# Clustered attention with an MLP: the small products of the q, k, v and x scales in even units behind the scores, and two tiles of the MLP's inner layer in one bank and pass

## The chip, the cores and the metric

The kernel runs on one core of a Trainium2 chip. TensorE (PE) multiplies, VectorE (DVE), ScalarE (ACT) and GpSimd (POOL) work elementwise, SyncE (SP) issues all transfers from one queue, in order. Each engine works through its own instructions in order. The metric is the time of one execution on the device, in microseconds (us); the figure for a kernel is the median of its runs.

## What is computed

Attention in which a query sees only the keys of its own cluster (the nearest of 16 centroids), and an MLP on its result:

```python
batch, n_heads, seq, head_dim = (4, 8, 768, 64)      # n_clusters = 16
q_assign = np.argmax(np.einsum('bhsd,hcd->bhsc', q_n, c_n), axis=-1)
k_assign = np.argmax(np.einsum('bhsd,hcd->bhsc', k_n, c_n), axis=-1)
mask = q_assign[:, :, :, None] == k_assign[:, :, None, :]
scores = scale * np.matmul(q, k.transpose(0, 1, 3, 2))
scores = np.where(mask, scores, -1000000000.0)
attn = softmax(scores)
x = np.matmul(attn, v)          # 3072 tokens x 512
h = x @ w_in                    # w_in 512 x 2048
r = np.maximum(h, 0.0)
out = (s * (r * r) + b) @ w_out # w_out 2048 x 512
```

Here q_n, k_n and c_n are q, k and the centroids divided by their norms. All inputs are float32.

## The kernel before

Float32 numbers are split into two float16 parts, hi and lo, after scaling by a power of two, and products are made of three matmuls of parts. The scale comes from the largest magnitude of a tile. DVE reduces along the free axis into a column `amb`, and a **small product** on PE (`allmax`, tile `am`) brings all 128 columns to every partition, where DVE reduces again.

The main loop runs over **units** i = 0 to 191, one per batch, pair of 128-row tiles of the queries, pair of heads, tile and head (`units`). In the timeline's names: `sc` are the scores of a unit (4 matmuls into one of two banks), `ssm` their maximum on DVE, `p` the exp on ACT, `ph` its hi part (ACT) and lo part (POOL), `PT` its transpose by DMA, `px` the product with v (`values`, in odd units for the two units five and four back), `xs` the divided result. Every four units `finish_x` makes `xn` (the hi and lo parts of `xs`) and its transpose `x`.

The MLP runs 21 units behind (`LAG`): step m = i - 21 takes one 128-wide tile `ft` of the inner layer for 256 tokens. Since 21 is odd, even steps m fall in odd units. `mlp_in` makes `h` (12 matmuls of 256 columns), `mlp_relu` makes `r` and the hi part of `g` on ACT, `mlp_gl` its lo part on POOL a unit later, `mlp_out` adds 6 matmuls of 512 columns into `acc` two units later. After 16 steps DVE makes `o` out of `acc`, and it goes out.

The inputs of later units are made by generators that `background` moves by one step at the end of every unit. `prep_q` (every 8 units), `prep_k` (four per batch) and `prep_v` (one per batch) load, take `absmax`, bring the scale round (`am`), split into hi (ACT) and lo (DVE), transpose (`QA`, `KA`), multiply with the centroids (`pq`, `pk`), make a one-hot row of the nearest on DVE (`om`, `oe`, `oo`, then `qb` or `kb`) and transpose again (`QB`, `KB`). For all pairs of heads after the first batch `kb` is one buffer: POOL copies the hi part of `ka` into it, DVE writes the one-hot beside it, and the KB transpose reads it.

`px`, `pq`, `pk` and `am` share one bank of PSUM (pool `ps_m`, tag m, one buffer). `h` has one bank too (`ps_h`), `acc` two as one buffer.

From unit 21 on (`pinned`) PE, DVE, ACT and POOL keep the order in which the code is written; SP's queue and everything before unit 21 are ordered by a scheduler.

## Time and profile before

| | us |
|---|---|
| median of 3 runs | 985.37 |
| lowest and highest | 985.28, 995.64 |
| profiled execution | 989.84 |
| its span, first to last instruction | 988.1 |
| matmuls on PE | 8625 |
| PE's mean granted clock, share of full | 0.932 |

The prediction shows lines of the profile. In a group of instructions stand the line of the code (L51 is the helper that records most instructions), engine, operation, output and inputs with shapes, count, busy us and mean ns of one, then the idle time of the engine ahead of them and what ended it. In a view of waits stand the waiting engine and tile, what it waited for, the sum in us, how often, and the longest. In a timeline stand start and length in us. A unit is called by its number i; the scores of unit 30 start at 207.16 us, those of unit 79 at 429.56, of 127 at 639.89, and of 191, the last, at 917.35.

### The profile page before, as it was taken

How to read it: one execution, taken by the hardware profiler on the slowest of the kernel's cores; microseconds unless marked ns; L12 is line 12 of the kernel's file. 1: busy time of each engine (PE TensorE's matmuls, PEld its weight loads, DVE VectorE, ACT ScalarE, POOL GpSimd, SP SyncE). 2: the span in 40 equal slices, each digit the busy share in tenths (PEclk: the TensorE clock that was granted, in tenths of full speed). 3: DMA queues.
4: the chain of work that ended last, by engine and by line, in shares of the span. 5: the costliest groups of instructions: out<-in, count | busy, mean ns of one | idle time of the engine just before them, and what ended most of it. 6: DMA issues, size and time to landing. Idle time of an engine off the chain costs nothing. (4 is left out here: it accounts for less than half of the span.)

```text
span 988.1 us, 22624 instructions
## 1 busy us (share of the span) xinstructions
PE 838.5 (85%) x8625; PEld 584.5 (59%) x8625; DVE 656.1 (66%) x1475; ACT 755.0 (76%) x1416; POOL 547.8 (55%) x543
## 2 busy tenths in 40 slices
PE   1576526787989999997899999997899999999997
PEld 0355315555566666675666776765566767667764
DVE  7798878898786655667876665676776556563200
...
GB/s 190 195 196 170 250 209 104 94 140 198 142 148 159 149 144 127 146 158 215 186 147 149 147 130 155 146 192 187 137 154 158 126 140 150 144 136 126 74 28 21
DMA packets 450300, 147.36 MB, mean 149 GB/s; under 512 B 417936, under 2 KB 446608, under 8 KB 450192
## 3 DMA queue, kind: packets, MB, share of 16 engines
...
## 5 line engine op out<-in xcount | busy, mean ns | idle before, releaser
L51 POOL TENSOR_TENSOR ph<-p,ph 128x768 f16<-128x768 f32 x184 | 308.1, 1675 | 80.1 <-ACT ph L51 55.1
L51 PE MATMUL h<-x,wis 128*128 128x256 f16 x2304 | 285.6, 273 | 12.6 <-ACT r L51 6.5
L51 PE MATMUL acc<-wos,g 128*128 128x512 f16 x1152 | 288.1, 387 | 0.8 <-POOL g L51 0.6
L51 POOL TENSOR_TENSOR g<-r,g 128x256 f16<-128x256 f32 x192 | 129.7, 676 | 276.4 <-ACT r L51 270.4
L51 PEld LDWEIGHTS <-wis 128*128 128x128 f16 x2304 | 226.4, 98 | 83.4 <-issue 17.6
L51 DVE TENSOR_REDUCE ssm<-sc 128x1 f32<-128x768 f32 x192 | 182.8, 953 | 102.0 <-PE sc L51 101.3
L51 ACT ACTIVATE p<-sc,ssm,qsm 128x768 f32<-128x768 f32 x192 | 189.9, 989 | 7.9
L51 PEld LDWEIGHTS <-g 128*128 128x128 f16 x1152 | 108.8, 100 | 109.2 <-issue 10.2
L51 ACT ACTIVATE r<-h,cf 128x256 f32<-128x256 f32 x192 | 89.9, 468 | 99.6 <-PE h L51 89.6
L51 ACT ACTIVATE ph<-p 128x768 f16<-128x768 f32 x174 | 143.9, 827 | 1.4 <-DMA KA<-ka 1.4
L51 PEld LDWEIGHTS <-PT 128*128 128x128 f16 x3312 | 117.7, 99 | 32.3 <-issue 22.9
L51 PE MATMUL px<-vh,PT 128*128 128x65 f16 x2208 | 121.2, 197 | 15.3 <-DVE qsm L51 7.9
L51 PE MATMUL sc<-KA,QA 128*128 128x384 f16 x384 | 101.4, 349 | 16.9 <-ACT p L51 14.0
L51 PE MATMUL px<-vl,PT 128*128 128x64 f16 x1104 | 115.1, 195 | 0.0
L51 ACT ACTIVATE ssm<-ssm,lift,qsm 128x1 f32<-128x1 f32 x192 | 72.2, 377 | 52.8 <-DVE ssm L51 51.9
L51 PE MATMUL sc<-KB,QB 128*128 128x384 f16 x384 | 101.8, 350 | 1.9 <-DMA QB<-qb 1.9
L51 ACT ACTIVATE g<-r 128x256 f16<-128x256 f32 x192 | 80.0, 417 | 6.1
L51 ACT ACTIVATE r<-r 128x256 f32<-128x256 f32 x192 | 80.0, 417 | 6.0
L51 PEld LDWEIGHTS <-QA 128*128 128x128 f16 x768 | 48.9, 100 | 28.2 <-issue 20.7
L51 PEld LDWEIGHTS <-QB 128*128 128x128 f16 x384 | 39.7, 104 | 31.2 <-issue 7.1
L51 DVE SCALAR_TENSOR_TENSOR o<-acc,xm,bias 128x512 f32<-128x512 f32 x24 | 16.9, 745 | 44.5 <-PE acc L51 44.4
L51 DVE TENSOR_SCALAR qsm<-qsm 128x2 int32<-128x2 int32 (+1 forms) x96 | 42.8, 446 | 2.2
...
## 6 DMA issues: line engine op xcount, KB each, us to landing
...
PT<-ph SPq DMA_TRANSPOSE x184, 3.5
x<-xn SPq DMA_TRANSPOSE x48, 2.9
```

Of the source, the lines that this page charges most:

```text
L51: ins = op(*args, **kw)
```

## The change

Four things are changed.

- **Where `allmax` stands.** In batches after the first, and for x, it is put on a list `soon` and made in the next unit, right behind the scores. For q and k the step of the generator that came before it is taken out, so that splitting and transposing come a unit earlier, and a step is put in before the products with the centroids, which keep their place in q.
- **Which units.** `prep_k` starts 3 units later, so that `am_k` and `pk` fall in even units, in which there is no `px`. `prep_v` starts 10 units later.
- **x.** `finish_x` is no generator any more. Its hi part and maxima are made in the odd unit, the rest (`am_x`, POOL's lo part, the transpose) stands in `soon`, ahead of POOL's other work of the even unit. It stood at the end of that unit.
- **The MLP in pairs.** In odd units `mlp_in` makes two tiles (24 matmuls) into the two halves of one bank, and one relu of 512 columns reads them. In even units ACT makes two squares of 512 columns, POOL one lo part, now behind `ph` of that unit, and PE the 12 matmuls of the pair before. `r` has one buffer for two, `g` two for four, of double size.

Two small tiles of the set-up (`ct`, `cnat`) change tags to fit.

Three places. First PE around the small product of q in unit 96 (`am_q2_0_1`; the second row of each pair is left out, `sc_97` and `sc_96` are scores). Before:

```order
L51 MATMUL h_1_1_11_7401<-x_19_6447,wis11_2267 128x256
L51 LDWEIGHTS amb_q2_0_1_7378
L51 MATMUL am_q2_0_1_7428<-identb_95,amb_q2_0_1_7378 128x128
L51 LDWEIGHTS QA_2_0_0_6936
L51 MATMUL sc_97_7435<-KA_2_0_6191,QA_2_0_0_6936 128x384
```

Now:

```order
L51 MATMUL sc_96_7075<-KB_2_0_6112,QB_2_0_0_6582 128x384
L51 LDWEIGHTS amb_q2_0_1_7073
L51 MATMUL am_q2_0_1_7083<-identb_95,amb_q2_0_1_7073 128x128
L51 LDWEIGHTS g_1_1_8_6933
L51 MATMUL acc_1_1_6466<-wos8_2031,g_1_1_8_6933 128x512
```

The product moved from the end of the unit to behind its scores, ahead of the 12 matmuls into `acc`.

Second DVE from the division in unit 95 (`xs_22`) to the maximum of the next scores. `amb_q` is what PE's `am_q` reads, `qsm` what DVE makes of it. Before:

```order
L51 TENSOR_TENSOR xs_22_7182<-px_90_7273,ssm_88_6733 128x128
L51 TENSOR_REDUCE om_k2_3_7372<-pk_2_3_7347 128x12
L51 TENSOR_TENSOR oe_k2_3_7373<-pk_2_3_7347,om_k2_3_7372 128x192
L51 TENSOR_REDUCE amb_q2_0_1_7378<-qn_2_0_1_7226 128x2
L51 TENSOR_REDUCE xm_20_6722<-xs_22_7182 128x1
L51 TENSOR_REDUCE ssm_96_7390<-sc_96_7383 128x1
L51 TENSOR_TENSOR oe_k2_3_7373<-oe_k2_3_7373,rev_73 128x192
L51 TENSOR_REDUCE om_k2_3_7372<-oe_k2_3_7373 128x12
L51 TENSOR_TENSOR oo_k2_3_7374<-oe_k2_3_7373,om_k2_3_7372 128x192
L51 TENSOR_SCALAR kb_131<-oo_k2_3_7374 128x12x64
L51 TENSOR_REDUCE qsm_2_0_1_7377<-am_q2_0_1_7428 128x2
```

Now:

```order
L51 TENSOR_TENSOR xs_22_6864<-px_90_6982,ssm_88_6461 128x128
L51 TENSOR_REDUCE xm_20_6428<-xs_22_6864 128x1
L51 TENSOR_TENSOR oe_k2_2_6966<-oe_k2_2_6966,rev_73 128x192
L51 TENSOR_REDUCE om_k2_2_6965<-oe_k2_2_6966 128x12
L51 TENSOR_TENSOR oo_k2_2_6967<-oe_k2_2_6966,om_k2_2_6965 128x192
L51 TENSOR_SCALAR kb_131<-oo_k2_2_6967 128x12x64
L51 TENSOR_REDUCE vm_2_6655<-vn_2_1_6752 128x1
L51 SCALAR_TENSOR_TENSOR ka_2_3_6975<-kn_2_3_6754,ksm_2_0_5981,ka_2_3_6975 128x12x64
L51 TENSOR_REDUCE amb_q2_0_1_7073<-qn_2_0_1_6905 128x2
L51 TENSOR_REDUCE qsm_2_0_1_7072<-am_q2_0_1_7083 128x2
L51 TENSOR_REDUCE ssm_96_7089<-sc_96_7075 128x1
```

The work of k and v that stood in other units now stands between the division and `amb_q`, and the maximum of the next scores stands behind `qsm`.

Third POOL around the copy into `kb` for the third pair of heads of batch 2 (`ka_2_2`). Before, in units 88 and 89:

```order
L51 TENSOR_TENSOR g_1_1_3_6759<-r_1_1_3_6757,g_1_1_3_6759 128x256
L51 TENSOR_TENSOR ph_88_6831<-p_88_6736,ph_88_6831 128x768
L51 MEMSET vh_2_0_6874 128x12x2
L51 COPY kb_131<-ka_2_2_6778 128x12x64
L51 TENSOR_TENSOR g_1_1_4_6862<-r_1_1_4_6860,g_1_1_4_6862 128x256
L51 TENSOR_TENSOR ph_89_6898<-p_89_6835,ph_89_6898 128x768
```

Now, in units 91 and 92:

```order
L51 TENSOR_TENSOR ph_90_6700<-p_90_6598,ph_90_6700 128x768
L51 COPY kb_131<-ka_2_2_6653 128x12x64
L51 TENSOR_TENSOR xn_21_6739<-xs_21_6546,xn_21_6739 128x2x128
L51 TENSOR_TENSOR ph_91_6764<-p_91_6704,ph_91_6764 128x768
L51 TENSOR_TENSOR g_1_1_6_6783<-r_1_1_6_6734,g_1_1_6_6783 128x512
```

The copy stood a unit behind the KB transpose that reads `kb` for the pair before; now both are issued at the end of the same unit. Behind the copy stands `xn`, ahead of `ph`, and `g` of double width at the end.

The core of the diff:

```diff
@@ -337,8 +339,9 @@
         km = columns(1, f"k{n}")
         absmax(km, kn.rearrange("p h t d -> p (h t d)"))
         if b:
-            yield
-        allmax(sm[1], km, f"k{n}", "m" if b or not hp else "h")
+            soon.append(lambda: allmax(sm[1], km, f"k{n}"))
+        else:
+            allmax(sm[1], km, f"k{n}", "h" if hp else "m")
         yield
         scale2(sm[2], sm[1])
         inverse2(V, sm[3], sm[2], 22)
...
@@ -353,6 +356,8 @@
         KS[(b, hp)] = (KA, KB)
         last_turn[0] = nc.sync.dma_start_transpose(KA, ka.rearrange("p h t e d -> p (h t e d)"))
         yield
+        if b:
+            yield
         yield
         pa = (ps_m if b or not hp else ps_h).tile([P, 512], F32, tag="m" if b or not hp else "h", name=f"pk_{n}")
         for h in range(2):
...
@@ -381,8 +386,9 @@
         qm = columns(2, f"q{n}")
         absmax(qm, qn.rearrange("p (j h) t d -> p j (h t d)", j=2))
         if b + c:
-            yield
-        allmax(sm[:, 1, :], qm, f"q{n}", "m" if b or c else "h")
+            soon.append(lambda: allmax(sm[:, 1, :], qm, f"q{n}"))
+        else:
+            allmax(sm[:, 1, :], qm, f"q{n}", "h")
         yield
         f = sm[:, 2, :]
         scale2(f, sm[:, 1, :])
...
@@ -405,6 +411,8 @@
         QS[(b, c, hq)] = (QA, QB, sm)
         nc.sync.dma_start_transpose(QA, qa.rearrange("p h t e d -> p (h t e d)"))
         yield
+        if b + c:
+            yield
         yield
         pa = (ps_m if b or c else ps_h).tile([P, 512], F32, tag="m" if b or c else "h", name=f"pq_{n}")
         for h in range(nh):
...
@@ -441,8 +449,9 @@
         vc = columns(1, f"v{b}")
         V.tensor_reduce(vc, vm[:, 0:NP], axis=AX.X, op=ALU.max)
         if b:
-            yield
-        allmax(vm[:, 5:6], vc, f"v{b}")
+            soon.append(lambda: allmax(vm[:, 5:6], vc, f"v{b}"))
+        else:
+            allmax(vm[:, 5:6], vc, f"v{b}")
         yield
         floor2(V, vm[:, 6:7], vm[:, 5:6])
         inverse2(V, vm[:, 7:8], vm[:, 6:7], 0)
...
@@ -570,16 +579,20 @@
         xn = sb.tile([P, CT, 2, 2, D], F16, tag="xn", name=f"xn_{g}", bufs=1)
         A.activation(xn[:, :, 0], xs, AF.Copy)
         absmax(XM[(b, c)][:, hp : hp + 1], xs.rearrange("p t h d -> p (t h d)"))
-        yield
-        G.tensor_tensor(xn[:, :, 1], xs, xn[:, :, 0], op=ALU.subtract)
-        x = sb.tile([P, CT, 2, P], F16, tag="x", name=f"x_{g}", bufs=9)
-        XS[(b, c, hp)] = x
-        nc.sync.dma_start_transpose(x.rearrange("p t e q -> p (t e) q"), xn.rearrange("p t e h d -> p (t e h d)"))
+        xm = XM[(b, c)]
         if hp == NP - 1:
-            xm = XM[(b, c)]
             xc = columns(1, f"x{g}")
             V.tensor_reduce(xc, xm[:, 0:NP], axis=AX.X, op=ALU.max)
-            allmax(xm[:, 5:6], xc, f"x{g}")
+
+        def rest():
+            if hp == NP - 1:
+                allmax(xm[:, 5:6], xc, f"x{g}")
+            G.tensor_tensor(xn[:, :, 1], xs, xn[:, :, 0], op=ALU.subtract)
+            x = sb.tile([P, CT, 2, P], F16, tag="x", name=f"x_{g}", bufs=9)
+            XS[(b, c, hp)] = x
+            nc.sync.dma_start_transpose(x.rearrange("p t e q -> p (t e) q"), xn.rearrange("p t e h d -> p (t e h d)"))
+
+        soon.append(rest)
 
 
     MS = {}
...
@@ -597,28 +610,34 @@
         V.scalar_tensor_tensor(xm[:, 7:8], xm[:, 6:7], xm[:, 6:7], glob[:, 6:7], op0=ALU.mult, op1=ALU.mult)
         MS[(b, c)] = [cf, xm[:, 7:8], None]
 
+
     def mlp_in(b, c, ft):
         n = f"{b}_{c}_{ft}"
-        ph = ps_h.tile([P, 512], F32, tag="h", name=f"h_{n}")
+        ph = ps_h.tile([P, 2, CW], F32, tag="h", name=f"h_{n}")
         GS[(b, c, ft)] = ph
         terms = [(kt, wl, xl) for kt in range(KT) for wl, xl in ((0, 0), (0, 1), (1, 0))]
-        for i, (kt, wl, xl) in enumerate(terms):
-            M.matmul(ph[:, :CW], WSP[ft][0][:, wl, kt, :], XS[(b, c, kt)][:, :, xl, :],
-                             start=(i == 0), stop=(i == len(terms) - 1))
+        for f in range(2):
+            for i, (kt, wl, xl) in enumerate(terms):
+                M.matmul(ph[:, f, :], WSP[ft + f][0][:, wl, kt, :], XS[(b, c, kt)][:, :, xl, :],
+                                 start=(i == 0), stop=(i == len(terms) - 1))
 
     def mlp_relu(b, c, ft):
         n = f"{b}_{c}_{ft}"
         ph = GS[(b, c, ft)]
-        r = sb.tile([P, CW], F32, tag="r", name=f"r_{n}", bufs=2)
-        A.activation(r, ph[:, :CW], AF.Relu, scale=MS[(b, c)][0])
-        g = sb.tile([P, 2, CW], F16, tag="g", name=f"g_{n}", bufs=4)
-        A.activation(g[:, 0, :], r, AF.Square)
+        r = sb.tile([P, 2, CW], F32, tag="r", name=f"r_{n}", bufs=1)
+        A.activation(r, ph, AF.Relu, scale=MS[(b, c)][0])
+        GS[(b, c, ft)] = r
+
+    def mlp_square(b, c, ft):
+        r = GS[(b, c, ft)]
+        g = sb.tile([P, 2, 2, CW], F16, tag="g", name=f"g_{b}_{c}_{ft}", bufs=2)
+        A.activation(g[:, 0], r, AF.Square)
         A.activation(r, r, AF.Square)
         GS[(b, c, ft)] = (r, g)
 
     def mlp_gl(b, c, ft):
         r, g = GS[(b, c, ft)]
-        G.tensor_tensor(g[:, 1, :], r, g[:, 0, :], op=ALU.subtract)
+        G.tensor_tensor(g[:, 1], r, g[:, 0], op=ALU.subtract)
         GS[(b, c, ft)] = g
 
     def mlp_out(b, c, ft):
...
@@ -627,12 +646,13 @@
             MS[(b, c)][2] = ps_a.tile([P, CT, DM], F32, tag="acc", name=f"acc_{n}")
         acc = MS[(b, c)][2]
         g = GS.pop((b, c, ft))
-        for t in range(CT):
-            rows = slice(t * P, t * P + P)
-            for gl, wl in ((0, 0), (0, 1), (1, 0)):
-                M.matmul(acc[:, t, :], g[:, gl, rows], WSP[ft][1][:, wl, :],
-                                 start=(ft == 0 and gl + wl == 0), stop=(ft == NF - 1 and gl == 1))
-        if ft == NF - 1:
+        for f in range(2):
+            for t in range(CT):
+                rows = slice(t * P, t * P + P)
+                for gl, wl in ((0, 0), (0, 1), (1, 0)):
+                    M.matmul(acc[:, t, :], g[:, gl, f, rows], WSP[ft + f][1][:, wl, :],
+                                     start=(ft + f == 0 and gl + wl == 0), stop=(ft + f == NF - 1 and gl == 1))
+        if ft == NF - 2:
             _, e, acc = MS.pop((b, c))
             o = sb.tile([P, CT, DM], F32, tag="stage", name=f"o_{n}", bufs=3)
             if b + c == 0:
...
@@ -665,8 +685,8 @@
                     at(s0, prep_q(b, c, hq))
         if b > 0:
             for hp in range(NP):
-                at(48 * b - 20 + 4 * hp, prep_k(b, hp))
-            at(48 * b - 16, prep_v(b))
+                at(48 * b - 17 + 4 * hp, prep_k(b, hp))
+            at(48 * b - 6, prep_v(b))
     splits = wsplit()
     wgen = weights()
 
...
@@ -737,6 +757,8 @@
         if i < NU:
             with first_of_all(i):
                 scores(i)
+        while soon:
+            soon.pop(0)()
         if due:
             with first_of_all(i):
                 px = values(i - 5)
...
@@ -754,18 +776,20 @@
             some(splits, 1)
         if 0 <= m < NS and steps[m][2] == 0:
             mlp_start(*steps[m][:2])
-        if 0 <= m - 2 < NS:
-            mlp_out(*steps[m - 2])
-        if 0 <= m < NS:
+        if m % 2 and 0 <= m - 3 < NS:
+            mlp_out(*steps[m - 3])
+        if m % 2 and 0 <= m - 1 < NS:
+            mlp_square(*steps[m - 1])
+        if m % 2 == 0 and 0 <= m < NS:
             mlp_in(*steps[m])
             mlp_relu(*steps[m])
-        if 0 <= m - 1 < NS:
-            mlp_gl(*steps[m - 1])
         if 0 <= i - 1 < NU:
             with first_of_all(i):
                 low(i - 1)
+        if m % 2 and 0 <= m - 1 < NS:
+            mlp_gl(*steps[m - 1])
         if due and (i - 5) % 4 == 2:
-            active.append(finish_x((i - 5) // 4))
+            finish_x((i - 5) // 4)
         background()
         if i >= LAG - 3:
             some(splits, 1)
```

More of the change, by code (lines that the diff above doesn't have):

```diff
@@ L87, in scale2 @@
         V.tensor_scalar(dst, dst, 2.0 ** 60, None, op0=ALU.min)
+    soon = []
     last_transpose = [None]
@@ L150, in behind @@
         return stack
-    ct = sb.tile([P, 2, D], F32, tag="r", name="ct", bufs=2)
+    ct = sb.tile([P, 2, D], F32, tag="r", name="ct", bufs=1)
     cn = ct[:, 0, :]
@@ L168, in tile_cluster_attention_mlp @@
     V.reciprocal(cs[:, 3:4], cs[:, 2:3])
-    cnat = sb.tile([P, 3, 2, D], F16, tag="r", name="cnat", bufs=2)
+    cnat = sb.tile([P, 3, 2, D], F16, tag="g", name="cnat", bufs=2)
     G.memset(cnat[:, 1:3], 0.0)
```

## The prediction

> **What bounds the kernel now.** I read the page's busy times first, then the windows, PE's waits, and the timeline where PE waits.
>
> ```profile
> PE 838.5 (85%) x8625; PEld 584.5 (59%) x8625; DVE 656.1 (66%) x1475; ACT 755.0 (76%) x1416; POOL 547.8 (55%) x543
> ```
>
> PE is the busiest engine, but it has 150 us without work. The windows tell where. I cut them at starts of scores: set-up; the first MLP steps while the weights are still split (units 21 to 29); then by turns the stretches in which the next batch's k and v are prepared (units 30 to 49, 79 to 97, 127 to 145) and quiet ones; last the tail without attention. Columns: stretch, its length, busy PE, PEld, DVE, ACT, POOL with counts, granted clock, DMA share, GB/s.
>
> ```profile
> 0.00:160.80 160.80, 77.70 (x612) 55.33 (x613) 133.28 (x303) 105.75 (x201) 75.57 (x90) 0.71 0.75 192
> 160.80:207.16 46.36, 37.51 (x386) 26.00 (x387) 39.49 (x74) 37.68 (x68) 25.57 (x22) 0.92 0.53 112
> 207.16:312.23 105.07, 90.06 (x974) 61.36 (x972) 86.14 (x188) 77.48 (x140) 57.71 (x54) 0.98 0.84 161
> 312.23:429.56 117.33, 112.74 (x1217) 79.71 (x1215) 70.23 (x159) 101.02 (x191) 73.04 (x70) 1.00 0.73 143
> 429.56:523.96 94.40, 82.95 (x921) 57.31 (x919) 73.23 (x170) 71.64 (x130) 54.18 (x53) 0.95 0.91 177
> 523.96:639.89 115.93, 112.86 (x1216) 79.66 (x1214) 70.92 (x159) 100.89 (x191) 73.07 (x70) 1.00 0.72 144
> 639.89:738.77 98.88, 85.78 (x920) 58.23 (x918) 73.31 (x169) 71.69 (x130) 54.74 (x53) 0.91 0.87 165
> 738.77:917.35 178.58, 174.27 (x1876) 123.45 (x1873) 100.91 (x230) 155.09 (x293) 113.10 (x107) 1.00 0.75 142
> 917.35:988.10 70.75, 64.63 (x523) 43.44 (x520) 8.60 (x25) 33.73 (x76) 20.78 (x28) 1.00 0.15 36
> ```
>
> Set-up is DVE's (133 of 160.8 us busy). In quiet stretches PE is 96 to 98% busy: nothing but PE's own work is left there. In the two later preparations PE is 87 to 88% busy, the clock falls to 0.95 and 0.91, and DVE is busiest after PE. What PE waited for from 160.8 us on:
>
> ```profile
> PE pk L51 <- DVE xs L51: 12.7, 7, 3.3
> PE am_x L51 <- DVE amb_x L51: 12.2, 10, 2.3
> PE px L51 <- DVE qsm L51: 7.9, 5, 2.2
> PE am_k L51 <- DVE oe_k L51: 7.6, 9, 0.8
> PE h L51 <- ACT r L51: 6.5, 6, 1.5
> PE h L51 <- DMA x<-xn: 6.1, 7, 1.5
> PE am_q L51 <- DVE ksm L51: 2.9, 3, 1.3
> ```
>
> The first four and the last are one thing: px, pk, pq and am all use bank m, and each must wait until DVE has read the one before. A quiet pair of units on PE:
>
> ```profile
> 361.76 0.49 PE L51 MATMUL sc<-KA,QA 128*128 128x384 f16 x2
> ...
> 362.41 1.46 PE L51 MATMUL acc<-wos,g 128*128 128x512 f16 x6
> 363.70 1.47 PE L51 MATMUL h<-x,wis 128*128 128x256 f16 x12
> 365.01 0.49 PE L51 MATMUL sc<-KA,QA 128*128 128x384 f16 x2
> ...
> 369.36 0.49 PE L51 MATMUL sc<-KA,QA 128*128 128x384 f16 x2
> ```
>
> An even unit takes 3.25 us (361.76 to 365.01): scores 0.65, acc 1.29, h 1.31. An odd one takes 4.35, with 1.1 for the values px. And a bad place:
>
> ```profile
> 451.02 0.75 PE L51 MATMUL pk<-cT,KA 128*128 128x16 f16 x24 [1.57 <-DVE xs L51]
> ...
> 461.00 0.23 PE L51 MATMUL am_x<-identb,amb_x 128*128 128x128 bf16 x1 [2.26 <-DVE amb_x L51]
> ...
> 463.34 2.54 PE L51 MATMUL acc<-wos,g 128*128 128x512 f16 x6
> ```
>
> After such gaps six acc matmuls take 2.54 us, not 1.46: a wait is paid twice. Lost by the clock in the four windows under 1.00 (length times what is missing): 3.7 + 2.1 + 4.7 + 8.9 = 19.4 us.
>
> **The change, part by part.** The profiled execution took 989.8 us for a span of 988.1; the median of the three runs is 985.4, so I make the sum on 989.8 and take 4.4 off at the end.
>
> *Two tiles of the inner layer in one bank and pass.* PE's matmuls keep number and size: 24 h in an odd unit (2.6 us), 12 acc in an even one (2.6), so 3.25 + 4.35 per pair as before. It saves on ACT and POOL:
>
> ```profile
> L51 ACT ACTIVATE r<-h,cf 128x256 f32<-128x256 f32 x192 | 89.9, 468 | 99.6 <-PE h L51 89.6 <-DVE om_q L51 3.3 <-PE am_k L51 1.8
> L51 ACT ACTIVATE g<-r 128x256 f16<-128x256 f32 x192 | 80.0, 417 | 6.1
> L51 ACT ACTIVATE wo<-wo 128x512 f32<-128x512 f32 x16 | 10.0, 622 | 6.8 <-DVE wo L51 6.8
> L51 POOL TENSOR_TENSOR ph<-p,ph 128x768 f16<-128x768 f32 x184 | 308.1, 1675 | 80.1 <-ACT ph L51 55.1 <-issue 4.6 <-DVE xs L51 3.0
> L51 POOL TENSOR_TENSOR g<-r,g 128x256 f16<-128x256 f32 x192 | 129.7, 676 | 276.4 <-ACT r L51 270.4 <-issue 5.4 <-PE px L51 0.4
> ```
>
> A 512-wide pass costs 622 ns where two narrow ones cost 834: about 0.2 us for the relu and 0.4 for the two squares in each of 96 pairs, 60 us of ACT; 512-wide g on POOL is halfway between 676 and 1675, 1.18 for 1.35, 17 us. Neither engine ends the path in quiet stretches, so I cost this at nothing; PE covers it, and without that cover it would be a gain. By the Trainium skill, "ScalarE: Activation LUTs", section on what ACT_TABLE_LOAD costs, a pass has a fixed 186 ns and 0.833 per element, an estimate of 613 for 512; the wo row agrees. "h waits for r" (6.5) falls in units 22 to 28. The bank now has an even unit and the next scores and px to come free (5 us, not 2). But DVE was busy 39.5 of 46.4 us there, and the wider h needs split weights a unit earlier: between 0 and 6.5 I take 2.2, near DVE's bound. r with one buffer: the relu waits for g on POOL, which ends about 3 us ahead in a quiet pair; no cost. Tail: last relu, two squares and g (0.7 + 1.24 + 1.18, some 0.4 between) stand against 2.6 of acc: +1.
>
> *x first.* am_x goes behind the scores of the even unit, at 0.65; its columns are ready some 3 us into the 4.35 of the odd one. The 12.2 go, from both kinds of stretch. POOL's xn stands ahead of ph (1.68) and g, so x lands earlier by more than the 1.5 that h waited: I take 5 of 6.1.
>
> *Small products in even units.* pk leaves the odd units, where it waited for the px just ahead: 12.7 go. am_k stands ahead of pk, not behind: 7.6 go. px behind am_q: 7.9 go, and the 2.9 of am_q. Together with the above 50.5 us of waits leave. Set-up: am and xn move a little under a scheduler; DVE bounds it (83% busy) and its work stays: 0, give or take 5.
>
> *What is late next.* am now stands ahead of 2.6 us of acc that would have covered it. What it waits for is DVE's queue:
>
> ```profile
> L51 DVE TENSOR_REDUCE ssm<-sc 128x1 f32<-128x768 f32 x192 | 182.8, 953 | 102.0 <-PE sc L51 101.3
> L51 DVE TENSOR_TENSOR xs<-px,ssm 128x128 f32<-128x128 f32 x96 | 27.9, 291 | 9.1 <-POOL xn L51 0.9 <-PE px L51 0.6 <-DVE ssm L51 0.5
> L51 DVE SCALAR_TENSOR_TENSOR ka<-kn,ksm,ka 128x768 f16<-128x768 f32 x16 | 19.0, 1187 | 0.0
> L51 DVE TENSOR_REDUCE amb_q<-qn 128x2 bf16<-128x512 f32 x24 | 16.3, 678 | 10.9 <-DMA qn<-in_q_dram 10.9
> L51 DVE TENSOR_REDUCE vm<-vn 128x1 f32<-128x768 f32 x16 | 15.0, 940 | 0.0
> L51 DVE TENSOR_TENSOR oe_k<-oe_k,rev 128x192 f32<-128x192 f32 x16 | 14.3, 891 | 0.1
> L51 DVE TENSOR_SCALAR ksm<-ksm 128x1 int32<-128x1 int32 (+1 forms) x64 | 9.1, 149 | 1.2
> L51 DVE TENSOR_REDUCE om_k<-pk 128x12 f32<-128x192 f32 x16 | 5.7, 356 | 16.8 <-PE pk L51 16.8
> L51 DVE SCALAR_TENSOR_TENSOR o<-acc,xm,bias 128x512 f32<-128x512 f32 x24 | 16.9, 745 | 44.5 <-PE acc L51 44.4
> ```
>
> Unit 95 (and 47, 143): from the end of pk in unit 94 DVE has om_k, oe_k, vm, four ksm, ssm, three small ones of the division (xs for each), five more between 0.36 and 0.89 (xm and the rest of the one-hot of k; the om_k row stands for those without a row here), vm, ka, amb_q: 0.36 + 0.36 + 0.94 + 0.6 + 0.95 + 0.87 + 0.36 + 0.89 + 1.08 + 0.94 + 1.19 + 0.68 = 9.2 us. PE asks for am_q at 4.35 + 0.65 and 0.3 of px waiting for oe_k: 5.3. A wait of 3.9. Unit 87 to 88 has the same queue without vm (7.3) but starts 0.9 later, behind two o (1.5, less the pk that PE does meanwhile): px waits 1.0, am_q 2.2. am_k at 86 and 90, where q's one-hot and products stand ahead: 1.1 together. px behind the other three pk: 0.4 each, 1.2.
>
> On POOL the copy of kb now stands in the unit in which the KB transpose ahead of it is issued, and must wait for it:
>
> ```profile
> KB<-kb SPq DMA_TRANSPOSE x16, 4.0
> ```
>
> In unit 91 DVE ends kb at about 5.5 (the queue above without vm, ka and amb_q), KB lands at 9.5, then copy, xn (1.7 together, by ph's row and their sizes), ph and g follow: g ends near 14.1, and acc of unit 94 asks at 13.0: 1.1. In 87 and 95 the am_q waits cover it. Sum per batch 3.9 + 1.0 + 2.2 + 1.1 + 1.2 + 1.1 = 10.5, for three batches 32. The lower end is 3.3 per batch, if DVE is always in time for am_q (rival A); the upper 17, if its lag carries on (B). I take what the rows add up to, since DVE's order is fixed there. px now always follows pq: +1, as seen in half of these units now.
>
> *Loads and queues.* The loads of k come three units later, of v ten. KB of the first pair of heads is issued in unit 39 for scores of unit 48, and v's first split is made in unit 51 for the px of unit 53: two units, 7.6 us, cover it, and a lag of DVE over that would show as px waiting. On SP the transposes of x now stand ahead of the same unit's PT; PT is read three units later. No cost for either.
>
> *Clock.* I keep 4.7 per preparation (the row 429.56, with 11.45 us of idle PE, is the nearest) and 2.7 early: 16.8 for 19.4, so -3. By the Trainium skill, "TensorE: Matmul & The Clock Gate", Part 1, only an idle window of about 3.4 us halves the clock; then only the 3.9 would be paid twice, some 6 us for three batches, and the sum would end at 953. The trace does not agree: in the bad place the longest gap is 2.26.
>
> Sum: -50.5 + 32 + 1 + 1 - 3 = -19.5; by windows (10 from the three quiet stretches, 8 from preparations, 2 early, 3 clock, -1 tail) -22. I take -21: 968.8, less 4.4: 964.
>
> **Rivals.**
> - A, DVE keeps up: its queue shortens because waits of PE let it catch up. New waits 10 for 32, clock 8 for 17: 964 - 31 = 933. For: DVE is only 74 to 82% busy in preparations. Against: its order is fixed, and om_k at its head waits for the end of pk.
> - B, the waits only change place: DVE's lag carries from 88 into 90 and from 96 into 98, per batch 17 for 10.5 and 2 us more clock: 964 + 25 = 989, no difference. For: the sum of DVE's work is the same.
> - C, slower: POOL's chain decides. If KB lands over 2 us later than I count (SP issues it behind a waiting PT), g, then the relu behind the one r buffer, then exp are late; 4 us and 1.7 of clock at nine places: 964 + 9 * 5.7 - 4 = 1011. It decides from KB landing after 11 us of its odd unit. Against: PE's own waits in 87 and 95 give it slack.
>
> **How the numbers follow.** Forecast 0.43 (950 to 975), A 0.25, B 0.21, C 0.11. The time is the forecast's, 964. The range takes in A and B and leaves out C: 930 to 988. Under 1% a measurement tells nothing: faster is below 975.5, forecast and A, 0.68; within 1%, B, 0.21; slower, C, 0.11.
>
> **What would show it.** Right: am_x and pk with no wait in quiet stretches, which are then some 3 us shorter each; ACT busy near 695; a wait of about 4 us at am_q of units 48, 96, 144, and about 2 at 88. POOL's kb waits for KB some 4 us in each preparation. Wrong: set-up longer than 166 us; acc waiting for g in quiet stretches; preparation windows of 80 us (A) or over 110 (C).

## The result and the profile after

The kernel got slower, by about 1%: a median of 1004.83 us (999.4 to 1005.89, 4 runs) against 990.11 (985.28 to 995.64, 4 runs) for the kernel before, a ratio of 1.0109 with a 95% interval of 1.0073 to 1.0144. The forecast was 964 us with a range of 930 to 988. The profiled execution took 999.4 us, the lowest of the four runs (the others took 1004.5 to 1005.9). It is set against the 989.8 of before: 9.6 us to explain, and 30.6 above the sum of 968.8; some 5 us more of the medians' difference stand in no profile.

First the busy times, then what PE waited for from the start of unit 21 at 161.8 us (waiting tile, what it waited for, sum in us, times, longest):

```profile
PE 840.6 (84%) x8625; PEld 579.9 (58%) x8625; DVE 680.3 (68%) x1475; ACT 697.1 (70%) x1128; POOL 527.5 (53%) x447
```

```profile
PE am_q L51 <- DVE amb_q L51: 23.9, 12, 3.9
PE am_k L51 <- DVE amb_k L51: 19.2, 10, 4.1
PE h L51 <- DMA x<-xn: 9.4, 5, 4.3
PE px L51 <- DVE oe_q L51: 3.8, 3, 3.2
PE px L51 <- DVE ksm L51: 3.6, 6, 1.0
PE px L51 <- DVE oe_k L51: 1.6, 6, 0.3
PE acc L51 <- POOL g L51: 1.1, 2, 0.7
```

Every wait that was to go is gone: am_x, pk behind xs, am_k behind oe_k, px behind qsm, h behind r (one am_x still waits 3.4 us at 160.7, in the set-up). In their place stand am_q and am_k, 43.1 us. ACT is 58 us less busy (the forecast said 60), DVE 24 us more, though it has the same 1475 instructions. The windows, cut at the starts of the same units as before (length; busy PE, PEld, DVE, ACT, POOL; clock; DMA share; GB/s):

```profile
0.00:161.81 161.81, 76.42 (x612) 53.86 (x613) 133.66 (x301) 104.73 (x199) 73.40 (x90) 0.71 0.72 189
161.81:207.81 46.00, 37.95 (x397) 26.75 (x394) 39.55 (x76) 36.04 (x58) 24.50 (x18) 0.89 0.53 113
207.81:316.10 108.29, 90.65 (x886) 58.03 (x884) 80.74 (x166) 67.25 (x106) 50.86 (x39) 0.94 0.74 153
316.10:439.40 123.30, 118.17 (x1299) 83.08 (x1298) 83.27 (x183) 97.04 (x153) 74.26 (x61) 1.00 0.67 142
439.40:530.44 91.04, 76.54 (x837) 51.81 (x836) 69.09 (x146) 61.43 (x97) 48.53 (x39) 0.96 0.86 176
530.44:649.90 119.46, 117.88 (x1299) 83.16 (x1298) 82.62 (x183) 96.96 (x153) 75.11 (x61) 1.00 0.73 142
649.90:746.20 96.30, 79.34 (x836) 52.97 (x835) 69.14 (x146) 61.37 (x96) 48.47 (x39) 0.93 0.81 170
746.20:927.20 181.00, 179.29 (x1957) 126.80 (x1956) 113.94 (x254) 146.56 (x232) 113.71 (x90) 1.00 0.68 141
...
```

Since work of k and v moved later, the quiet stretches carry some that stood in the preparations, and a preparation and the stretch behind it are to be read together: 207 to 439, 231.6 us for 222.4; 439 to 650, 210.5 for 210.3; 650 to 927, 277.3 for 277.5. The loss shows in the first of these; in the later two the gain and the loss cancel. The clock lost 5.1 + 6.5 + 3.6 + 6.7 = 21.9 us (length times what is missing), against 19.4 before and 16.8 forecast.

One bad place close up, units 93 and 94: DVE first (start, length, what it did), then POOL, then PE.

```profile
506.39 0.29 DVE L51 TENSOR_TENSOR xs<-px,ssm 128x128 f32<-128x128 f32 x1 [0.72 <-POOL xn L51]
506.60 1.50 DVE L51 TENSOR_TENSOR oe_q<-oe_q,rev 128x128 f32<-128x128 f32 x1
...
508.46 0.81 DVE L51 TENSOR_TENSOR oo_q<-oe_q,om_q 128x128 f16<-128x128 f32 x1
509.30 1.61 DVE L51 TENSOR_SCALAR qb<-oo_q 128x512 f16<-128x512 f16 x1
510.83 0.94 DVE L51 TENSOR_REDUCE amb_k<-kn 128x1 bf16<-128x768 f32 x1
```

```profile
504.90 0.82 POOL L51 COPY kb<-ka 128x768 f16<-128x768 f16 x1 [5.46 <-DMA KB<-kb]
505.68 0.67 POOL L51 TENSOR_TENSOR xn<-xs,xn 128x256 f16<-128x256 f32 x1
506.31 1.64 POOL L51 TENSOR_TENSOR ph<-p,ph 128x768 f16<-128x768 f32 x1
507.91 1.20 POOL L51 TENSOR_TENSOR g<-r,g 128x512 f16<-128x512 f32 x1
509.07 3.33 POOL L51 TENSOR_TENSOR ph<-p,ph 128x768 f16<-128x768 f32 x2
```

```profile
511.83 0.23 PE L51 MATMUL am_k<-identb,amb_k 128*128 128x128 bf16 x1 [3.29 <-DVE amb_k L51]
511.90 4.13 PE L51 MATMUL acc<-wos,g 128*128 128x512 f16 x12
```

am_k stands behind the scores and asks at 508.5. Its column amb_k is the last thing in DVE's queue of unit 93 and comes at 511.8; ahead of it three small operations of q's one-hot (oe_q, oo_q, qb) took 3.9 us. Each of them ends 0.15 to 0.18 us after the instruction that POOL had running: ph ends at 507.95 and oe_q at 508.10; g at 509.11 and oo_q at 509.27; the first of the two ph that follow (half of 3.33 us) at 510.73 and qb at 510.91. The reduction amb_k, beside the second ph, takes 0.94 as always. The 12 acc behind the gap take 4.13 us for 2.6, and the granted clock is 0.50 from 513.1 to 516.5.

DVE's queue is not all of it. The load of `kn`, which amb_k reduces, goes out at 504.94 and lands 4.5 us later, at 509.4. With DVE free at that moment amb_k would have come at 510.4, so of the 3.3 us that am_k waits some 1.9 are the load's and 1.4 DVE's (an estimate from these times). At units 46 and 142 the load lands 0.5 and 1.2 us before DVE begins amb_k. By the same estimate 7.1 of the 10.2 us that am_k waits in units 46, 94 and 142 are the load's. For am_q in units 48, 96 and 144, which wait 3.6 to 3.9 us each, the load had landed 4.4 to 6.7 us before amb_q began: there it is DVE's queue alone.

### The profile page after: what moved, and what is told of

It reads as the page before. It is cut to its first block, busy times and chain, and to the rows that moved or that the text cites. A ratio compares the mean times of both kernels' runs of the same rounds, so it can differ in the third digit from the quotient of the medians.

```text
span 997.7 us, 22123 instructions
## 1 busy us (share of the span) xinstructions
PE 840.6 (84%) x8625; PEld 579.9 (58%) x8625; DVE 680.3 (68%) x1475; ACT 697.1 (70%) x1128; POOL 527.5 (53%) x447
## 4 chain that ended last, share of the span: by engine, by line
PE 57%; DVE 13%; issue 4%; POOL 3%; ACT 2%; DMA 2%; SPq 0%; POOLq 0%; DVEq 0%; ACTq 0%
PE acc L51 22%; PE h L51 17%; PE px L51 8%; PE sc L51 7%; POOL ph L51 2%; DMA x<-xn 2%; DVE ssm L51 1%; DVE oe_k L51 1%; DVE vl L51 1%; DVE qa L51 1%; DVE amb_k L51 1%; PE pb L51 1%; DVE wos L51 1%; DVE om_k L51 1%; DVE o L51 1%
## 5 line engine op out<-in xcount | busy, mean ns | idle before, releaser
L51 PE MATMUL h<-x,wis 128*128 128x256 f16 x2304 | 271.1, 274 | 9.4 <-DMA x<-xn 9.4
L51 PE MATMUL acc<-wos,g 128*128 128x512 f16 x1152 | 277.9, 393 | 1.1 <-POOL g L51 1.1
L51 PEld LDWEIGHTS <-wis 128*128 128x128 f16 x2304 | 220.7, 98 | 37.7 <-issue 10.5
L51 POOL TENSOR_TENSOR g<-r,g 128x512 f16<-128x512 f32 x96 | 111.8, 1164 | 157.4 <-ACT r L51 156.8
L51 PEld LDWEIGHTS <-g 128*128 128x128 f16 x1152 | 114.0, 101 | 130.3 <-issue 15.9
L51 ACT ACTIVATE r<-h,cf 128x512 f32<-128x512 f32 x96 | 65.8, 686 | 113.0 <-PE h L51 93.0
L51 PE MATMUL sc<-KA,QA 128*128 128x384 f16 x384 | 99.2, 342 | 16.2 <-ACT p L51 13.3
L51 PE MATMUL sc<-KB,QB 128*128 128x384 f16 x384 | 99.4, 344 | 1.9 <-DMA QB<-qb 1.9
L51 POOL TENSOR_TENSOR xn<-xs,xn 128x256 f16<-128x256 f32 x48 | 34.0, 708 | 55.6 <-ACT xn L51 39.5
L51 ACT ACTIVATE r<-r 128x512 f32<-128x512 f32 x96 | 60.5, 630 | 3.1
L51 ACT ACTIVATE g<-r 128x512 f16<-128x512 f32 x96 | 59.4, 619 | 0.3
```

What stands on the lines that cost most here:

```text
L51: ins = op(*args, **kw)
```

## The experiments

Kernels are named by what they are: "before" and "after", and the three parts of the change: x (am_x and xn first), pairs (the MLP), qkv (small products of q, k and v behind the scores, k and v later). A ratio is to the kernel before in the same session, with its 95% interval.

### What the waits are: e1, e2, e5, e8

Two theories. Theory 1: POOL, held by the KB transpose, works off its backlog just when DVE makes q's one-hot, and DVE's operations stretch beside it. Theory 2: am waits because amb is last in DVE's queue of the unit just ahead.

**e1**: kb twice.

```diff
-        kb = kb_kept
-        if b == 0 and hp > 0:
+        if b or not hp:
+            kb = sb.tile([P, 2, T, 2, D], F16, tag="kb", name=f"kb_{b}_{hp}", bufs=2)
...
```

> The kernel after, with two buffers for kb instead of one (the room comes from vh and vl, 4 buffers each for 5; v comes so late now that the fifth is not needed). Theory 1, POOL's backlog: in the kernel after POOL waits 50.0 us (9 times) for the KB transpose before it may copy kb, then works its queue without a pause while DVE does the one-hot of q; DVE's operations stretch (1.50 us for oe_q, 1.61 for qb in unit 93), and am_k at units 46, 94 and 142 waits 3.3 to 3.5 us for it. Then here: POOL's kb waits under 5 us in all, oe_q and qb of unit 93 near 0.3 us each, am_k of 46, 94, 142 under 0.7 us, and three half-clock units less: 10 to 20 us less than the kernel after (985 to 995). Theory 2, DVE has too much to do in its fixed order whatever POOL does: am_k there still over 2.5 us, the time within 4 us of the kernel after (1000 to 1008). Under both am_q of 48, 96 and 144 still waits 3 us or more.

Measured: 1000.0 us, 1.0081 (1.0052 to 1.0110), not told apart from the kernel after. POOL's waits for KB, 50.0 us in the kernel after, are gone. am_k waits 14.1 us for 19.2 (1.5 for 3.3 in unit 94, but still 3.4 in 46), and am_q 30.6 for 23.9 (4.9 for 3.9 in unit 96, where ka, ahead of amb_q, takes 1.53 us for 1.01 beside POOL's ph). The time is in theory 2's range. What POOL's stall costs in one place comes back in another. It does not show that DVE's order alone holds am_k: in units 46 and 142 DVE now stands idle 1.8 and 1.3 us until the load of kn has landed.

**e2**: am of q, k and v behind acc (shown for k; the same for q and v).

```diff
-            soon.append(lambda: allmax(sm[1], km, f"k{n}"))
+            late.append(lambda: allmax(sm[1], km, f"k{n}"))
...
         if m % 2 and 0 <= m - 3 < NS:
             mlp_out(*steps[m - 3])
+        while late and i % 2 == 0:
+            late.pop(0)()
```

> The kernel after, with the small products of q, k and v made behind acc of the even unit, not ahead of it (those of x stay behind the scores). Theory 3, the place alone exposes the waits: 2.6 us of acc then cover them, am_q (23.9 us) and am_k (19.2) fall to under 10 together, the units of 8.7 to 9.2 us go, and the time is 25 to 35 us below the kernel after: 970 to 980. Rival, the waits only change place: ksm and qsm come 2.6 us later, the px of the odd unit that follows waits for DVE to empty bank m (px behind ksm or qsm over 15 us in sum), and the time is at most 10 us below the kernel after.

Measured: 987.2 us, 0.9959 (0.9928 to 0.9989); by the difference of the ratios, as in the runs that follow, 15 us below the kernel after: between the two. am_q and am_k fall from 43.1 to 3.9 us, but pk, next in the bank and now without cover, waits 15.8 for ksm and vm, px 6.4 for qsm, acc 7.2 for g.

**e5**: only amb and the load ahead of it one unit earlier (shown for k; the same for q).

```diff
         absmax(km, kn.rearrange("p h t d -> p (h t d)"))
         if b:
+            yield
             soon.append(lambda: allmax(sm[1], km, f"k{n}"))
...
-                at(48 * b - 17 + 4 * hp, prep_k(b, hp))
+                at(48 * b - 18 + 4 * hp, prep_k(b, hp))
```

> The kernel after, with the loads of q and k and the maximum of their magnitudes (amb_q, amb_k on DVE) one unit earlier; am itself, the splits and all the rest stand where they do in the kernel after. Theory 2, am waits because amb is the last thing in DVE's queue of the odd unit just ahead: am_q (23.9 us) and am_k (19.2) fall below 5 us together, without any cover by acc, and the time is 25 to 30 us below the kernel after, 970 to 978. Rival, DVE is late as a whole: then what stands behind amb in its queue is late in its place (px behind ksm, qsm or oe over 15 us, pk or pq waiting for DVE), and the time is at most 10 us below the kernel after.

Measured: 975.7 us, 0.9844 (0.9807 to 0.9882), 26 us below the kernel after. PE's waits in it:

```profile
PE am_v L51 <- DVE amb_v L51: 10.6, 3, 4.2
...
PE am_k L51 <- DVE xs L51: 2.2, 1, 2.2
PE am_q L51 <- DVE xs L51: 1.8, 2, 1.0
```

am_q and am_k stay in their place and wait 4.0 us in all. DVE has no less to do (685.7 us busy for 680.3). So theory 2's time and waits came out. But two things moved, the maximum and its load. For am_q, whose loads had landed long before in units 48, 96 and 144, this shows that the order of DVE held it. For am_k of units 46, 94 and 142 the load would have held it too, and no run moves the one without the other. What is left are am_v, the product whose maximum was not moved, px behind ksm, oe_q and qsm (11.7), and acc behind g (9.0).

**e8**: POOL's lo part of ph in four pieces.

```diff
-        G.tensor_tensor(u["ph"][:, 1, :], u["p"], u["ph"][:, 0, :], op=ALU.subtract)
+        n = 4 if i >= 30 else 1
+        for z in range(n):
+            zs = slice(z * S // n, (z + 1) * S // n)
+            G.tensor_tensor(u["ph"][:, 1, zs], u["p"][:, zs], u["ph"][:, 0, zs], op=ALU.subtract)
```

> The kernel after, with POOL's lo part of ph made in four pieces of 192 columns instead of one of 768 (from unit 30 on; about 0.5 us more POOL time per unit). Theory 1, an operation of DVE of the kind that was stretched (oe_q by rev, qb, qa, vl, ka, oe_k by rev) stands still until the POOL instruction that runs has ended, not until POOL's queue is empty: with pieces of 0.5 us it waits at most that long; their means fall (qa from 982 to about 550 ns, vl from 1918 to about 1200, oe_k by rev from 1141 to about 700), DVE is 15 to 25 us less busy, am_k of units 46, 94 and 142 waits under 1.5 us, and the time is 5 to 12 us below the kernel after. Theory 2, the waits come from DVE's fixed order: the means may fall, but the time stays within 4 us of the kernel after. A third way: DVE is held for all of POOL's busy time, so pieces change nothing in the means or make them longer.

Measured: 991.7 us, 0.9999 (0.9974 to 1.0024), 11 us below the kernel after, DVE 38 us less busy. Groups of DVE (count, busy us, mean ns, idle before) in the kernel after, then here:

```profile
L51 DVE TENSOR_REDUCE ssm<-sc 128x1 f32<-128x768 f32 x192 | 182.7, 952 | 86.0 <-PE sc L51 84.1
L51 DVE SCALAR_TENSOR_TENSOR qa<-qn,qsm,qb 128x256 f16<-128x256 f32 x44 | 40.6, 961 | 0.0
...
L51 DVE TENSOR_TENSOR oe_k<-oe_k,rev 128x192 f32<-128x192 f32 x16 | 16.1, 1004 | 0.1
```

```profile
L51 DVE TENSOR_REDUCE ssm<-sc 128x1 f32<-128x768 f32 x192 | 182.7, 952 | 96.9 <-PE sc L51 96.0
L51 DVE SCALAR_TENSOR_TENSOR qa<-qn,qsm,qb 128x256 f16<-128x256 f32 x44 | 25.0, 606 | 0.0
...
L51 DVE TENSOR_TENSOR oe_k<-oe_k,rev 128x192 f32<-128x192 f32 x16 | 9.0, 563 | 0.1
```

The reduction ssm keeps its 952 ns; qa and oe_k, with two inputs in SBUF, lose 37 and 44%. Others of this kind gain less or lose (ka 1160 for 1291, oo_k 661 for 500). So theory 1 is right in that DVE stands until POOL's instruction ends, and its time came out. Its waits did not: am_k of units 46, 94 and 142 was to wait under 1.5 us and waits 5.5, 2.4 and 3.6. DVE ahead of am_k of unit 46 (start, length):

```profile
295.93 0.52 DVE L51 TENSOR_SCALAR qb<-oo_q 128x512 f16<-128x512 f16 x1
301.19 0.96 DVE L51 TENSOR_REDUCE amb_k<-kn 128x1 bf16<-128x768 f32 x1 [4.74 <-DMA kn<-in_k_dram]
```

DVE is in time here and waits for the load of k, as it does 2.4 us for unit 94 and 3.3 for 142. am_q of 48, 96 and 144 still waits 3.4 each behind DVE. Moving amb and its load (26 us, e5) is worth more than shorter holds (11 us).

### What each part is worth: e3, e4, e6, e7, e10, e13, e14

Each part alone or left out; the edits are those pieces of the diff of the change.

> The kernel before, with the change to x alone (am_x behind the next unit's scores, xn on POOL ahead of ph, the transpose of x earlier; MLP, q, k and v as before). The prediction's steps for x: am_x behind amb_x goes from 12.2 us to 0 and h behind x from 6.1 to about 1, the time 12 to 20 us below the kernel before. Rival, the waits only change place: am_x now takes bank m ahead of the px of the next odd unit, and what PE gains there it loses at px, pk or h behind r: within 6 us of the kernel before.

> The kernel before with the change to q, k and v alone (small products behind the scores of even units, pk and pq in even units, loads of k and v later; x and the MLP as before). If the parts add up, the kernel after without pairs (ratio 0.9989) less x alone (0.9822) leaves 1.7% for this part: a ratio of 1.013 to 1.021, with am_q and am_k behind amb 30 us or more. The prediction had this part as even (31 us of waits gone, 32 new): a ratio of 0.997 to 1.005. A third way: it is the meeting of both parts that costs (x's products and transposes in the same units), and the part alone is under 0.995.

> The kernel before, with the pairs of the MLP alone (two tiles of the inner layer in one bank and pass; x, q, k and v as before). Theory A, the pairs are harmless and cost or give nothing, since ACT and POOL do not end the path: ACT busy near 695 us, time within 6 us of the kernel before. Theory B, they are what made the kernel after slow (acc or h in one long piece wait for a buffer, am in the odd unit stands behind 24 h): 10 us or more over the kernel before. Theory C, they are worth something by themselves (h waits less for r and for x): 5 to 12 us below it.

> The kernel after without the pairs of the MLP (one tile of the inner layer per unit again; the small products, x, k and v as in the kernel after). Theory A, the pairs are harmless: within 6 us of the kernel after, and am_q of 48, 96, 144 still waits over 3 us. Theory B, the pairs make the new waits worse, since they put 2.6 us of acc behind the small product where there was 1.3 of acc and 1.3 of h: 10 us or more below the kernel after.

> The kernel before with x first and the pairs of the MLP, without the change to q, k and v. Theory, the pairs cost by themselves 0.6 to 1.2% wherever they stand: against x alone (ratio 0.9822) 6 to 12 us more, a ratio of 0.987 to 0.995. Rival, what they cost was the wait of h for x, which an early x takes away, and the am of even units with 2.6 us of acc behind it, which is not here: a ratio of 0.979 to 0.985, h behind x under 5 us.

| kernel | parts | us | ratio |
|---|---|---|---|
| e6 | x | 973.2 | 0.9822 (0.9785 to 0.9859) |
| e13 | qkv | 1009.2 | 1.0168 (1.0120 to 1.0217) |
| e3 | pairs | 998.4 | 1.0056 (1.0030 to 1.0082) |
| e4 | x, qkv | 992.5 | 0.9989 (0.9961 to 1.0016) |
| e14 | x, pairs | 965.1 | 0.9730 (0.9688 to 0.9772) |
| after | x, pairs, qkv | 1004.8 | 1.0109 (1.0073 to 1.0144) |

e6 came out as the steps for x had it, e13 as the parts that add up, e4 as theory B. e3 is within theory A's 6 us, but above the kernel before all the same. e14 missed both its ranges: it is faster than theory and rival.

x gives 1.8% (0.0178 of 990, 17.6 us). qkv alone costs 1.7%, and x and qkv add up to within a thousandth (1.0168 - 0.0178 = 0.9990, measured 0.9989; the intervals are some 0.003 to 0.005 either way). The pairs depend on their company: +0.6% alone, -0.9% with x, +1.2% with x and qkv. In e13 the two waits that qkv makes are there without any help:

```profile
PE am_k L51 <- DVE amb_k L51: 26.6, 11, 4.6
PE am_q L51 <- DVE amb_q L51: 17.1, 9, 3.2
```

Why do the pairs cost when they are alone? PE in unit 53 of the kernel before, then of e3 (px left out):

```profile
324.81 0.49 PE L51 MATMUL sc<-KB,QB 128*128 128x384 f16 x2
...
326.22 1.46 PE L51 MATMUL acc<-wos,g 128*128 128x512 f16 x6
327.52 1.15 PE L51 MATMUL h<-x,wis 128*128 128x256 f16 x9
330.21 0.49 PE L51 MATMUL h<-x,wis 128*128 128x256 f16 x3 [1.54 <-DMA x<-xn]
```

```profile
327.94 0.49 PE L51 MATMUL sc<-KB,QB 128*128 128x384 f16 x2
...
329.36 1.15 PE L51 MATMUL h<-x,wis 128*128 128x256 f16 x9
332.95 3.33 PE L51 MATMUL h<-x,wis 128*128 128x256 f16 x15 [2.45 <-DMA x<-xn]
```

Before, 6 acc stand ahead of h in the odd unit. With pairs acc is in even units only, h follows px at once and starts 1.42 us after the last scores for 2.71, 1.3 us sooner; x lands 5.0 us after them for 5.4. h waits 15.6 us for x in e3, against 6.1. (The wait is paid twice: after a gap of 2.45 us 15 h take 3.33, where 12 take 1.47 in the kernel before; the granted clock is 0.50 meanwhile.) With x first the same order waits 0.7, as e14 shows, and h's waits for r (9.4 in e6) and acc's for o (5.8) are gone: the pairs gain.

> The kernel before with the pairs of the MLP alone, once more, for its profile. In the first run of it h waited 15.6 us for x (10 times), against 6.1 in the kernel before, and the time was 0.6% above it; the same is expected: 13 to 18 us at h, and am_x, pk and am_k as before.

e7 is e3 once more: 998.1 us in one run, h 16.2 us behind x, pk 10.7, am_x 12.2. e10 has the older x:

```diff
-    LAG = 21
+    LAG = 23
```

> The kernel before with the pairs of the MLP alone, and the MLP 23 units behind the attention for 21 (two units more for x to land; the last steps come two units later, the first too). Theory, what pairs cost is that h stands first in the odd unit behind px, where half of acc (1.3 us) stood ahead of it, and so asks for x earlier: h behind x falls from 15.6 to under 1 us, and the time from 0.56% above the kernel before to between 0.5% below it and 0.2% above. Rival, x is not what costs: the waits of h for x go and the time stays at 0.4% above or more.

Measured: 999.2 us, 1.0082 (1.0053 to 1.0110): the rival's words, not the theory's time. h no longer waits for x, and the last unit of attention starts 4.3 us sooner than in e3 (918.8 for 923.1 us), but am_q waits 10.0 for ksm where it waited 1.9, px 14.0 for qsm for 7.4, and the MLP's tail holds 24 more h. A lag moves more than x, so this run does not rule the theory out, but it does not bear it out either. For it speaks e14: with x early the pairs gain. That the wait for x is all of the pairs' 0.6% is not shown.

### Looking for the best version: e9, e11, e12, e15 to e18

All but e17 and e18 have qkv with early maxima (as e5, amb_v too). e9: no pairs. e11: lag 23. e12: that and ph in two pieces. e15: the small products between the two halves of acc. e16: that and two pieces. e17: x and pairs, without qkv, and prep_k one unit earlier, which puts pk and am_k behind acc in even units. e18: that and two pieces.

```diff
+            while f and late:
+                late.pop(0)()
...
-            at(48 * b - 6, prep_v(b))
+            at(48 * b - 7, prep_v(b))
...
-                at(48 * b - 20 + 4 * hp, prep_k(b, hp))
+                at(48 * b - 21 + 4 * hp, prep_k(b, hp))
```

(The first piece is that of e15 and e16, in mlp_out's loop over f; the second that of e9, e11, e12, e15 and e16, with a step more ahead of v's small product; the third that of e17 and e18.)

> The kernel after without the pairs of the MLP, with the loads and the maxima of q, k and v a unit earlier (amb_q, amb_k, amb_v; the small products stand where they do in the kernel after). Theory, the pairs cost by themselves: the kernel after without pairs was 1.2% below the kernel after, so this comes out about 12 us below the same with pairs (ratio 0.984 to the kernel before), at a ratio of 0.965 to 0.976, 956 to 967 us; h waits under 2 us for x. Rival, the pairs cost only through the waits of am, which had 2.6 us of acc behind them: with am in time there is no difference, a ratio of 0.980 to 0.988.

> The kernel after (pairs too), with the loads and maxima of q, k and v a unit earlier and the MLP 23 units behind for 21. Against the kernel after with early q and k alone (ratio 0.984; there h behind x 4.3 us, am_v 10.6 us): both go to under 1 us, with the half clock behind the am_v of 4.2 us: 10 to 18 us less, 956 to 966. Rival, an older x changes nothing but the ends: tail and start cost what the waits gave, 970 to 976.

> As the run with early maxima and the MLP 23 units behind, and POOL's lo part of ph in two pieces of 384 columns. In the kernel after four pieces took 38 us off DVE's busy time and about 11 us off the time. If DVE's held operations still decide (px behind ksm, qsm and oe_q, 12 us in sum), two pieces give 2 to 6 us more; if not, POOL's longer work (acc behind g, 9.0 us) takes it back and it is 0 to 5 us slower than without pieces.

> The kernel after (pairs, 21 units), with the loads and maxima of q, k and v a unit earlier and their small products between the two halves of acc in the even unit (those of x behind the scores). With the maxima early alone the ratio to the kernel before was 0.984; there am_v waited 10.6 us for amb_v and am_k, am_q 4.0 for xs. Theory: 1.3 us of acc ahead covers the waits for xs, 1.3 behind lets DVE empty the bank ahead of pk: am under 3 us in sum, pk behind ksm and vm under 3 us, and 8 to 15 us less: a ratio of 0.970 to 0.977. Rival, DVE or POOL are late as a whole by now (acc behind g 9.0 us, px behind oe_q, ksm and qsm 11.7): the waits move there and the ratio is 0.980 or more.

> As the run with the small products amid acc, and POOL's lo part of ph in two pieces. Two pieces took 28 us off DVE's busy time at an MLP 23 units behind (695.9 to 668.3) and 2 us off the time. Expected the same here: DVE 20 to 30 us less busy, 0 to 4 us less time than without pieces; if it gives more than 6 us, DVE's held operations are what bounds the preparations.

> The kernel before with x first, the pairs, and the preparation of k one unit earlier (start at 48b - 21 for 48b - 20), so that pk and am_k come at the end of even units, behind 2.6 us of acc, without being put ahead of it. q and v as before. With x and pairs (ratio 0.973) pk waited 11.6 us for xs, am_k 7.6 for oe_k. Theory: even units are the right place, the place ahead of acc was the fault; pk behind xs falls below 2 us, am_k behind oe_k stays, 8 to 14 us less: a ratio of 0.959 to 0.966. Rival, any move of k into even units brings DVE's queue to PE (pq, am_q or the px of the odd unit behind ksm and oe_k over 12 us): a ratio of 0.975 or more.

> As the run with k one unit earlier, x first and pairs, and POOL's lo part of ph in two pieces of 384 columns: 10 to 30 us less of DVE's busy time, and 0 to 5 us less time, as the two pieces gave in two other places (2 and 3 us); slower by 2 us or more if POOL's longer work now reaches acc (acc behind g over 6 us).

| kernel | us | ratio | |
|---|---|---|---|
| e9 | 976.1 | 0.9842 (0.9815 to 0.9868) | the rival: as e5, which has pairs; h 1.0 behind x, but acc 23.2 behind g, h 11.3 behind r |
| e11 | 971.6 | 0.9807 (0.9772 to 0.9842) | the rival's time; no wait of h for x, but am_v 9.9 behind xs, am_k 8.0 |
| e12 | 969.7 | 0.9782 (0.9757 to 0.9807) | DVE 668 for 696 us busy, 2 us less time, within the intervals |
| e15 | 984.1 | 0.9932 (0.9902 to 0.9962) | the rival, and worse than e5: acc 17.7 behind g, px 10.2 behind qsm |
| e16 | 980.9 | 0.9895 (0.9869 to 0.9921) | 3 us less than e15, DVE 20 us less busy; within the intervals |
| e17 | 966.2 | 0.9765 (0.9732 to 0.9798) | the rival's time, not its waits (px 3.4 behind ksm and oe_k); pk's wait for xs gone, am_k 10.6 behind oe_k, h 6.8 behind x: no gain on e14 |
| e18 | 965.6 | 0.9740 (0.9693 to 0.9788) | as e14; DVE only 5 us less busy than in e17 |

The best is e14, the change without its qkv part: 965.1 us, 2.7% below the kernel before. Its waits:

```profile
PE pk L51 <- DVE xs L51: 11.6, 9, 3.4
PE am_k L51 <- DVE oe_k L51: 7.6, 9, 0.8
PE px L51 <- DVE qsm L51: 7.3, 4, 3.2
```

These are the waits that qkv was made to remove; e17 removes the first without putting am ahead of acc, and gains nothing by it: of these 11.6 us am_k and h, waiting for oe_k and x, take back 9.1, and px behind qsm 1.8.

## Why the prediction was wrong, by its own steps

The terms of the sum, and the same terms in the profile after:

| term | forecast, us | measured, us |
|---|---|---|
| waits that leave: am_x, pk, am_k, px, am_q | -43.3 | -43.3 |
| new waits: am_q, am_k, px, acc (53.2, less 3.2 of the same kinds before) | +32 | +50.0 |
| h behind x (6.1 before) | -5 | +3.3 |
| h behind r (6.5 before) | -2.2 | -6.5 |
| clock | -3 | +2.5 |
| set-up | 0 | +1.0 |

The measured column adds up to 7 of the 9.6 us, and 2.6 stay unaccounted for; of the forecast, two terms of +1 are left out.

**Two tiles in one bank and pass.** Right for ACT (697.1 us busy, about 695 forecast) and for g on POOL (1.16 us for 1.18). Wrong in "PE covers it": the step looked at what the pairs save and not at what they move. That acc leaves the place ahead of h, and with it 1.3 us of cover over x, was in the order and was not counted. Alone the pairs cost 0.6% (e3), where h waits 9.5 us more for x.

**x first.** The size came out where x is alone: forecast 12.2 + 5 = 17.2, measured 17.6 (e6), and both waits went. In part it is luck: px and pk wait 7.5 us less behind qsm, oe_q and xs, while px behind ksm, am_q behind ksm, h behind r and acc behind o wait 13.4 more, and PE is 8.8 us less busy. In the full kernel h waits 9.4 us for x after all. The step "On SP the transposes of x now stand ahead of the same unit's PT" took only PT into account. SP's queue and POOL at unit 133, whose scores start at 674.29 (start, length, line):

```profile
671.74 1.40 SPq L357 DMA_TRANSPOSE KA<-ka  x1
673.30 3.00 SPq L536 DMA_TRANSPOSE PT<-ph  x1
676.35 0.57 SPq L104 DMA_DIRECT2D kn<-in_k_dram  x1
677.03 1.19 SPq L593 DMA_TRANSPOSE x<-xn  x1
```

```profile
670.84 1.55 POOL L51 COPY kb<-ka 128x768 f16<-128x768 f16 x1
672.36 0.66 POOL L51 TENSOR_TENSOR xn<-xs,xn 128x256 f16<-128x256 f32 x1
```

In e14 the same x goes out before its unit begins (scores of 133 at 654.31):

```profile
649.97 0.67 POOL L51 TENSOR_TENSOR xn<-xs,xn 128x256 f16<-128x256 f32 x1 [0.66 <-ACT xn L51]
653.23 1.19 SPq L585 DMA_TRANSPOSE x<-xn  x1
```

In the kernel after x goes out 2.7 us into the unit and lands 4.7 us later, and h waits 4.3 us, the longest of all. In e14, where k's preparation stands as in the kernel before, it goes out 1.1 us ahead of the unit and lands 3.6 us later. Of these 4.9 us 2.4 arise on POOL, where xn stands behind the copy of kb and ends 1.3 us ahead of the unit for 3.7. SP's queue adds 1.4 (the KA of k, a PT and a load of k go out first) and the transfer 1.1.

**What is late next.** This step carries most of the error: 32 us forecast, 50.0 measured. The queue of DVE was the right place to look, and where it was added up it came out: 3.93 us at am_q of unit 96 for a forecast of 3.9, 2.27 at 88 for 2.2, px 1.00 at 87 for 1.0. What failed is its scope.

- Units 21 to 53 hold 24.7 us of the 53.2, units 82 to 99 hold 12.4 and units 130 to 147 hold 12.7, for a forecast of 10.5 each. The step took the first preparation to be like the others. In these units am_k of 34 waits 4.15, am_q of 24 3.35 and px of 29 3.23 (1.89 before). In unit 33 two operations qa, 2.26 us together, and a split of weights, 0.75, stand ahead of amb_k on DVE; neither was in the sum.
- am_k of 46, 94 and 142 (3.3 to 3.5 us each, with half clock behind) was not in the sum either. DVE's queue was late there, with 3.9 us for three operations of 0.3 each beside a busy POOL, and so was the load of k.
- Against that, the 1.1 us of acc behind g per batch did not come.

So 32 became 50, the clock term went from -3 to +2.5, and the part that was to come out even costs 1.7% alone (e13). That the order of DVE holds am_q is shown by e5 with the landing times; for am_k it is DVE's order and the load together. What held operations cost in all is 11 us (e8).

**Loads and queues.** "No cost for either" was wrong in both halves. The step asked of the later loads of k only whether KB comes in time for its scores. It did not ask whether kn comes in time for amb_k, now that am_k asks right behind the next scores and not at the end of that unit: some 7.1 us at am_k of 46, 94 and 142. The other half, x on SP, is told above.

**POOL's copy of kb, and the rivals.** The copy waits for KB 50.0 us in all, 4.5 to 7.0 each, as the step said of its place. This wait does not decide the time: without it the time is not told apart (e1). So rival C, whose time of 1011 is near the 1004.8 measured, was right about the time by another way than its own. Rival B, the waits change place, comes nearest in mechanism. Its 17 us per batch, 51 in all, is near the 53.2 measured, but by luck: no lag carried from 88 into 90 (0.3 us) or from 96 into 98 (none), and nearly half of the waits stand in units 21 to 53. Its end at 989 leaves out that h waits 9.4 us for x. Rival A is out: DVE is late where it was to catch up.

**Clock.** The prediction kept the row's 2.26 us gap against the rule of the Trainium skill ("TensorE: Matmul & The Clock Gate", Part 1) that an idle window of about 3.4 us halves the clock. By that rule, the 2.45 us gap in unit 53 of e3 would have cost nothing behind it; the trace does not agree: 15 h took 3.33 us there, at a granted clock of 0.50. The step was right to keep the row, and the number of such gaps was wrong.

Open is why the pairs, which gain 0.9% with x, cost 1.2% once qkv is there too. The waits of h for x (9.4 us, 1.4 without pairs) and of am_k (19.2, 13.5) rise, those of h for r and acc for g (7.4 and 7.3) nearly go; with the 4.5 more that px waits for oe_q and ksm, and 0.3 less at am_q, that is 4.6 us of the 8.7 between the two spans. No run takes it further apart.
